# Second MLP, first pair of tiles: its output products as one single-precision matmul each, in an order found anew

## The chip, the cores and the metric

The kernel runs on one core of a Trainium2 chip. The metric is the device time of one execution in microseconds (us): the median of several runs, lower is better. The rows below come from one profiled execution, whose own time is given beside its span.

## The reference, cut to what matters

Attention over a causal window of 128 positions (4 batches, 8 heads, 576 positions, 64 per head) gives 2304 tokens of 512 numbers. A first MLP (512 to 2048 to 512, leaky activation with a slope for each hidden unit) and then the second MLP follow, all in single precision:

```
h = np.maximum(np.maximum(x @ w1, x @ w2), x @ w3)     # 2304 x 512 times 512 x 768, three times
return (h @ w_out).astype(np.float32)                  # 2304 x 768 times 768 x 512
```

## The kernel before

**Products of rounded parts.** TensorE takes operands in a rounded 32-bit form (`F32R`, shown as fp32r in the rows). To keep the precision, an operand is split in two: a rounded high part (ScalarE, a cast) and the rounded rest (VectorE or GpSimd, a subtraction), by the helper `split` (L519 to L524). A product is then three matmuls, high by high, high by rest and rest by high, added up in PSUM. Operands that are not split, those of the attention's scores (L872), transposes (L931) and values (L951, L968, L975), go to TensorE as plain single precision (`F32`).

**Second MLP.** `second_mlp` (L1082) goes through the tokens in tiles of `TILE` = 384, two tiles at a time, so there are three pairs (`p` = 0, 1, 2). The hidden products of a pair are block products (`product`, L1216) of 384 columns. For pairs 1 and 2 the output product is done by blocks too (`outs_by_blocks`). Only the first pair, p = 0, takes the plain way: `outs` (L1244) is called 18 times, for 2 tiles x 3 blocks of 128 tokens x 3 pairs of hidden chunks, and each call does two chunks `j` with three matmuls each, 128 tokens by 512 outputs. Its stationary operand is `g[j]`, the hidden values that `close` (L1435) splits when a maximum is complete. Its moving operand is `Wo[j]`, the output weights that `last_weight` (L1206) loads into a buffer of the ring `wt` and splits into one of the slots `WO_AT`.

**Attention.** `pair` (L812) handles two heads and 256 queries: 8 calls of the score matmul (L872), softmax on VectorE (L903), ScalarE (L909) and GpSimd (L921), 6 transposes (L931, the tiles `p` by the identity), a copy of the transposes from PSUM to the tile `pt` on ScalarE (L939), then the values (L951 reads `pt`), and a copy of the result (L998 or L983, ScalarE). Scores, transposes and values of most pairs share the ring `sb` of two PSUM banks, and `pt` is a ring of one. The last pairs run between the hidden products (L1034 to L1036) and output products (L1062) of the first MLP.

**Order.** Every operation is recorded by `plan.add` with an engine, a planned cost and its operands. `Plan.issue` (L137) then takes the operations in the order of a table of numbers, `ORDER`, and the DMA queue on SP and each engine get their instructions in that order. Between TensorE operations that the plan has early in the program, `keep_busy` (L161) puts fill matmuls (L461) on the identity; another 24 stand in the program from `pair` (L455).

Of the kernel before, what the change touches and what calls it, by code (L numbers as in the profile page):

```python
# [11 lines left out]
F32 = mybir.dt.float32  # L12
# [7 lines left out]
B, H, S, D = 4, 8, 576, 64  # L20
T = B * S
# [3 lines left out]
P = 128  # L25
# [3 lines left out]
NJ = DF2 // P  # L29
NC = NB // 2  # L30
N = 2 * P

R = 3 * D
# [56 lines left out]
class Plan:  # L90
# [162 lines left out]
    'c-'  # L253
    'jrqgJO_t007X>#$Ro<Y^)ZxW!tuG+qP}nwr$(CZQgs{;UGXka*zZNP!c2qB|tII9&ms`TaXfz1|0wc5(tn2Yy?Sx0}2FS7tkOk@E'
    '`^V0jWT05F5k-'
    'rNCTJ9E1V`o`N(W3}gUtfCX_u8ITF22k}5g5Dub1S#Sbm1_?lX5D5~3b^w5AkO<@j??6Y86{H1OKw^*$R0Ng5CXgLe0r|imPz_W7'
    'IY3TO3Df{pK^Kq<YytT}Zcqyp09!#5P#qKmdBA3{4MfA5U>;}+dV}qt4%iJMKwnTE3<UAu0#F<D2X#SbPzdY=MZgYF7}NvhKv9qm'
    '>;rv3H_#Jw0u4Y9&=2ec9btFS3p4{=L4D8=bcKUKb8r%j2HjvIFa$gUEx>*-'
    '01O51!C%lA3<58}7|;?72gAU8&>D;dAHg^P!3fX_j0Af?8!!bd1mnRduoOH8i@^af4J-mvL2|eZyaeUpbg&$p0-'
    'wMHa2iYkufP(p0!#$2!3;1NtORSpLGS?#hne9yFcXZ1v%xB`4!i-gz-llD`~zn|0=OO=1{XjLxCWdBhrk$k5o`dLz<F>7WI&$*fS'  # L260
    '17)a0JAMU%*vx6x;y!z%j5KR)h)RHE<Ig2VcQ0a2KS6iQshrVPkY3aCjTUfCy6f03?R7U^c`chDjiSS>Z$Q7zp?l#DrO3QWy!d!4'
    'Q}Oo`%_BE*J{)z})Z=cmi_5WH1Wmh2Ow;kPjAuv7v<dVP{wvhQT<n089ZDj0=lE3oF0~*a;SdHDM~~U{P2LriLwGCiDYn*b-'
    'KPt>91KVQbh1RffMn8)#s9I1@ERRbUSE8w9W!%mCZMs<1t52M?i)umdax7oje&1RMb~!D=uKY!2I@;;<(ShuvXG_#XC!y<rbn3Z6'
    '!NV0G9F)`p{CKez(cf&F1wH~<cYrC~WZ5)OoE;Sg8`4u#|4O4tz2Mq}Y1I1z@Rac~%%3@5>Ka0#3MZ=<>}Bbo~v!Fq5hTn4AYDR3'
    '2xMD<}~cm~ddP2e;*4`xTx;Vjq`E`qb+Ubq(Shcn<3v=Od{bKpU^8t#MZ;AXf6Zh{Bke7FIgg;D4PTmT!uCul3&0vE$*bP^ter(j'
    'NW2xdk*VH30vo`XlwHkb?DMcd&nm<8oV$6*+G2p_|za5uaT&!V#AGTZ?#!e?j?JP#kiCom7X3NOJ6@D)4^ufdP-'
    '2z&#tzz;Afc?R>M*RUFChTg&F(4(yAEqnow!cXu9Y>sZiyD%SWi(bNb<QBXK6>5P5VrUk+4JG;tOQQSmH%v}AYKiirX5=R<Pc-'
    '@rf5G;oJ*q+OK!d)(R_Hr?0AnMII-qYb25ODwkUua$4lPC<Q4!RFgrWkd6GEsf`T=91m}m~_j0&Q^up^m^FzSK|p*UzB`3DJ_hYl'
    'lvx*>{+q6icZL6jEtLWxj(G#{l$2~dBO7^OqKQ4$n}5~5-#DO!r+qN8X5+JH)<!l(pVN=l*PXdz04lA-SC3@U?;p&lqTT85ING-'
    'x?mjT)l*C<R(hj-#?D992c-'  # L270
    'P(_pyH9`YXd9(sGKwnS=v=LQCJy8|(6`eq9P#?4sT_TmxO(bbQv<jU>15jVI7TrO&&^J^KokG>oAXFQzL-$Y(^c3AkHBlXOg*-'
    'r4&{R|x4M)?FrlV0UG!zX+_0UK(3{68r&_gr>jY6^T2o!?HpiSr;dW6=a@8}cSf^L)ZXft|@V$!i_BD#P+qjBgex`?)-'
    'N$5Gcgx;d@=o;FFCZiqbF4>MIpq=O^x{fZRUnqo5L9y`*6qnpUp*R`cg_4n%C<fk*-'
    'l09{6^e=Dlh^1y+Kb+x4=4pmK|i95cpo}|%8~u(AWBKXZ~_t+S0F!7LXr<xB<W}-'
    'oQV8J2>(F<8=M>eMUglf=fM!CBL7e&f^ifkI5iPCGfqq>mN*VhPc3FR4M~f;&?KZQRX855PMYCFnBxRE3)Z+fPJ$iIi{s<UBpXhQ'
    'b6}6t;jB0zu7zuooH#oUa4wt_N8n^Q6%Hp=NPe6ir^d-'
    '~Ez+E%!Bt6BoC0US9Y_mY2#>;*a5yf8E91hr1Wt)Z<07~?u1yNyqPQg~h)d$exDKg?OW~Hd9IlO<;PSXMu7aE5R-'
    '_K@M(dIaxH|4m%itQgHK~Ye;<C6CX@$q&y0{H#i0hHQxF2py+TwM1F6oTh<Mp^BZigG;dbksAjXRSLxD6hT+mSA~KOTU);`w9*9*'
    'et>k+>)BhU?=6q!-?Rmyv~}0q%~+;of*4?ty#IK6nM`Nr&P=xGPzN7vhO{FrJKW;;DENUPPwjTX-'
    '5Cf`{SpcnV%gCg2%(HC{z#;>CC_UV^)kS$H1ah}YuTcn$7O7L)n-'  # L280
    'GFd|A;7#}rxk?t`rT8|!Mpoiwcr`hOkK)~UIo^u@;+=RK{)e~YRrosDg*W3J_#WAUui+K=2HAs;<GuI<K8SDNJNP=jPu7rq_z(u<'
    'CV4>i<F({2K8#OdMGxR!^cLw&&*BgG2!4b=;%7J(eMlbQ%;X7vh)>}x<SG7z4ZVjS<4}4Y|HhWy$Fb=j{0Tey97FN~$DwcVY5a)1'
    '#GbyzXYe_E0l&flMdUHLh~MGl^fkVOW6&!&l*A_QF((mJldNPAp+u4}%E(}H8DGVUU?NCLN=PIzBm<2@EJ;N_;}|50#3YVnBdKXL'
    'iA!UVjMS5OG&>0)nP?yS1qWmZ=}Uj$T%;69LraqaBsa-Nc91+IKlzG>(48bN`H6Fof}{}1Ns5vF<QtBpg-LNzhJ@3!<U1Zp29UIL'
    'Ac>+yNC^^6hmoQr9Vtn6kq9!BW+ds!Xfl$_B(um^GKP*K@5p$Pfs7;X$yPFk3@5|r1X7<2rz6OAGJ<X+v&l$0kxV7K$s{t3OeUl0'
    'bTW!gA(_Yw(tvy*dq_jlkM^gHNMq83Tp;_&d2*DDr3c7Cl9wJPhe$qpgft~n=w5Q193%V4YjT=gB;#lg@|K(+XUKT^k-Q-'
    '%$pm_qOr{g*DRPc{B0WidI*IloeMxWfn|vjVa{7~eBem#v(ue#awP`={gG{BL$sh8C<f4BGqW=h{f&#jZ<fhYT0h)&rI-No~gHk%'
    '1&ZGtDdQykZp#$g!GLUX28%Ys5ix#6*XjNK@7NzHC3A%|Cr|0PwQj!*;WoT(ymKLVfX*pVf)}<9`dHRIZpp|GfT9a0$_2^vslsqF'
    'BXngvd%%ctI655e=qRnX|`kOYTjcGIbhrS?9Xni`LwxA1W1A3aaq-|*edXZ+PXK6dyigu<6X?uExwx)yVLOPgspl#@4`j;-'
    'EmuME6mA)j`=~McgKBHG@Qucygqc`bonvC6`ugGP3i{7PI=nr~_-lO+vBKnUep%3UUnwb8iOX)-'  # L290
    'UhywPQE~ClWa+;LJVoxY#p)7>0p_t{MMHy#=#b%NfV}h-qj6t@NDu!4hrkQ6cST<@{P8u-FlCV`YJB`5-'
    'vy;@Z)ifq6&Qh|q^b}3Ya<c4f3(dvSuy?c-'
    '%fZ4~1{T3uvvh17O~ul)^)wSp%{I_NEF+6#8)*ranZ2h`tT4;MHq)%E2s=Wf*$4WGZlY~iHujNzrX|@?x|JTIFX?ewiS41~SRGc6'
    ')n(&Y8Fqq}W#d@|R-Tn&_1QLBk+o&b*>+lmRc5bfX%>goU@h1V+LG<2ujvH#hVG<QSxxqq)?(FII~K-'
    'v(b}v!i_3Dec&sz)&IYnUtRrjBy0T6zKI_1`vAuL6>%zX!!E7|k!+Nj=Y#;5(#<09>Ec;6Pvi-Cl>%|Vx-'
    's~VfOeeAatRd^e2Czo#5S_}Fv88M_o5rTI$!sQ@!Pc|oY!;is=CV0#9-Gg;(T!{aYseR{1Z*K|!56W`>^oh;HnB#$F;B>v@Xf3#-'
    '@;n)X1pce#+vhdtN?4xx3V3q4bRWEvkts1Z^ygyovc3}!iMo(Y&UDqJMvDvGk;;a@E*J?@5%SDUVI?$#s~1;ybmwPM)2W$DC^6|@'
    'uqALAI2K9!F(j2%7^e#ya^l1`|)OMG#|sq^O0-'
    '<pUCI(;cOD0%tx^4d<mbzr}43T1|P*{@>zTZo6Xno`FtK<z!&mmd=X#D=kUdRIp54z@RfWmTgO+jReU#J%h&S(auu5<H}KVLFWbl'
    'u@vVFlU&FTW)qES@!w1TBY&+k}ckq3Du-wOX@<VKh+|N(({p<jrE)TGw@*um&kMP5MkUYYU@?HEOKgMUu<NPq2A&;^X{205*PqNe'  # L300
    'eI6KSF@DuDLKgZAW2mBJhz%TPt><Yiiukp+5JiExQ^B4Ry8zFD8vuv2W!LP94@;$%BZ?FsOHXkJ~v61o-'
    'zsVl*Gwcq3$?vnP>=i%9?($jkF~7$juxso#yU#!HXY3<?!mqR0@*(@qpYqrI4tvJm@aOC<`^4Y!@$xOZ$KLTd@)7&TKl2ytF?-'
    'JE${+kEf5N!<!r!r{>?{AmUNRu&$u$y+_v{s0AV*6lg!sm#m@i+muj~VxD1WmzY^j_iKeBJ^6Z0YvNc`es<RA8%ua)1~PWhRQmFw'
    'gW_LE`$hyP-KIpJ6=lz-WBIa$UQE94ZZ_##R9KekvB0eBoiMVQbW@|7|MM|_oJJfSdroMeLY2~zNwT=MlYj9b1$CK8E7EUtv(Q>E'
    'vdWWeL{5WZE$<1xer8OpVY&6mkIe4|Xv<MX84hy>h<ggl8jBNOo?JQ+{L<BF6bIZrB5@OUB(k13LglsvhJCE|<JJVa#Vsl;lTT7>'
    'fiB0{7QX?c3SS%!*mk%_0{nMGQWfp3$Me2a|WxkP4uR;Cb9e7oEsqj`Ffg=Y}EWLAD&W)$f}7Lir#k(oqpaZctD-'
    '((??jb{^kWu(Z?vx_KkLH?9^MGl@r<P#U=KADr36nS~HC@k`eBI1b5&2x(VG8fO!3y6IDfGjGCiN5NRJSa<vJiN3hE)K~uqM|4vc'
    'FP*#s4OcE%YveuxGb;80=&F9CV$BW;<)@R3-'
    'X7ulBg`2i<;tutRSk0+M<@IDjv&|@{z128j3pNs;n*w@mI33I3??fm!^rRC$7m?rm1KlZplWXy*Mqe%h$4-xFP?^R-&b-'
    'FPe#)^1Cd|Z_7{ehwLEwi952RD8lc`*5ZroB-'  # L310
    ')7XqO)i#?#Uivfa)n;$|tgm7_54UuHwENDte2jvYmJ!Kg&L%zZf8%$)fy?94ns7uX3O$#^1^pa*7zJ28lm%u;?q^$w6wE7%r&#E8'
    'oj;Vu%20gfOZ&{~)27Am)gVlBw~+si^`ft4i>Z0;`E)ln7Om1XrU4QPYG_lSNxKS0q-`g;euIY_(X-'
    '5c7psW5i6cKqObQgi@=;LJ_EvT&qQ*pDM)@sTiui+9YDC*&?BerIv_YVyRdr+NtGYjaVT<)G)PHtP?B69JOAQ=9@)QwMA?Y2SpsU'
    'QLGYMMVLyWwuv%)yGW*Xh?8Qsh^zLBOlqIlBjTwGV!s%!!qrZ3Kt!q$Duv3S;;XdkhDfOrs6!%^IxM2pDUnl^<wwLBky;%U<@i}~'
    'Or%pq)H!inq*13uggP(UtBaz5O0O=7`{Jg!B`%9-bz7VeS44SUNM%qR)E$voT@}woMs-aLQQ1`mo<$8+S=BpHP(2WL#dYyeWK;J<'
    'E;U~jR*%Fnm0LX)PsBHoM?Dp#)C-'
    'YUy%euRQT19>RDVTjHCH_oZ$v&dPgUfVRWVhGzZb>T2eClqSCv!=byAg4AH`cyQhgUyR9Ur9{Sf~IkW5xppG0L|PJI^T)lcz7R8v'
    's?5><Ew#pQ1y<X2H$A^Ar*DJ7Ol)>K4>N-'
    'd47p%ThKR^?t&Sxd!`F=aI#OU9A0Wr(!0wn{9+WJ(!V#*^`7gsi6$$t1EmPax~6q%xVzEK|wkGPO)2Yw+|kTsBl0WLlX~rjsdTCY'
    'f8-'  # L320
    'QIWE#ijrAmA(>TXlZ{k%nL{>HIc2nLtn$d_s+7ztYw~=uu*@%u$XdLp9H|P(VltO3C|jyZvbe0TO2`&!l&UF9%QCX8Y^9p0a<aUv'
    '%}dILvVt6=D$6Res;tAS$=0f(9H+*r>awM*C2Ppqa*C=W+o<uXuB;~~sQR*l9IYD3iE659EStzls;R8Yo5@A0m7J!U%X<8jnyebg'
    '*7CHPu9m1Ca<S^DW~er@t7<Dd%2jHn>Lk0V`h2PCt~RR9a+d0$R;y*Ivzo1rt4^wc+N64_cCx2ju1=_4s+ZiQx~Mg(0q-'
    'JLsP?jjT&p&#-m<Igt#+%Gs+;Vi)~R!<x$Yy^tG=?O?kBgX4Qi+AF1M=wa+^A%_NeV@uiBvwt9|OM+OMvt^Xh;)sxGL5>Z-'
    'b^j;L$uy1K1ysGI7Lx}$EXyXum<te&WQs;R!On(4>tfqJT1=&AaldZUW!N2-'
    ';6rrxRN>V<l%UaD8>gL<vrtG4>1YOUMpPpXZcre|oNr|ZwEub!#r>Sg+i`l04&sJ|+yzp0;UzMiGOtHB!S+4`4KdWc@GyJ?|U>fd'
    'UP?ygtsJ-UmIsaNRs`j1+y*J-'
    'W$=~x=;uDZYet2*dan&=q%pQ1WMchpQT(VcWJ&9%{?+UoWCfnKVej<0*`&U&NXpoi+%x{pq#z22nb=oGq#4s-'
    '&&K!@q!db3`rlk0@Kr;e)=>6CheUZmsc0Xnfxr3dM~I*DGR2kO*1sotme>svaFKA_j?F?yt)pu_brJxZt3WAza|QIFGGbOwD;kJi'
# [1340 lines left out]
```

## Time and profile before

| | us |
|---|---|
| median of 3 runs | 772.17 (771.73 to 773.33) |
| the profiled execution: its time | 773.07 |
| the profiled execution: its span, first to last instruction | 771.3 |

The page of the profile gives the busy time of each engine as a share of the span: TensorE's matmuls (PE) 98%, its weight loads (PEld) 86%, VectorE (DVE) 75%, ScalarE (ACT) 58%, GpSimd (POOL) 37%. Matmuls are pipelined: a row's duration reaches past the start of the next matmul, so that what one matmul costs is read from start to start.

### The profile page before, as it was taken

The page shows a single profiled execution, that of the slowest core. Times are in us where ns is not written, and L with a number is a line of the kernel's source. Part 1 is how long each engine was busy: PE and PEld are TensorE (multiplying, and loading weights), DVE is VectorE, ACT ScalarE, POOL GpSimd, SP SyncE. Part 2 cuts the span into 40 slices and gives each one's busy share as a digit, 9 for nine tenths or more (in the row PEclk, how much of TensorE's full clock was granted, in tenths as well). Part 3 has the DMA queues.
Part 4 walks back from the last instruction along what each step waited for, and adds up shares of the span by engine and source line. Part 5 has one row for each costly group of instructions (what it writes and reads, how often), then busy time and mean ns, then how long its engine had stood idle before and what let it go on. Part 6 is the DMA issues. An engine that isn't in the chain of part 4 may idle for free.

```text
span 771.3 us, 17302 instructions
## 1 busy us (share of the span) xinstructions
PE 756.8 (98%) x6018; PEld 664.8 (86%) x6022; DVE 575.8 (75%) x1457; ACT 447.8 (58%) x1235; POOL 284.5 (37%) x385
## 2 busy tenths in 40 slices
PE   7899999999999999999999999999999999999998
PEld 4689877878777789988888888899998999999997
DVE  6999989987566689979785759669865676824574
ACT  5999867766454546468865756455445434422251
POOL 5655647667545344366553413413332200000000
PEclk9999999999999999999999999999999999999999
DMA  9877556555655476366877936787986999697502
GB/s 305 287 237 240 181 176 245 169 200 188 212 182 178 162 239 215 91 197 182 267 226 242 374 130 222 286 292 263 355 290 218 288 368 387 191 313 240 192 2 83
DMA packets 93096, 175.75 MB, mean 228 GB/s; under 512 B 11088, under 2 KB 53712, under 8 KB 93008
## 3 DMA queue, kind: packets, MB, share of 16 engines
q1 hardware_dynamic: 92544, 174.11, 68.3%
q8 instruction: 48, 0.79, 0.5%
q10 hardware_dynamic: 464, 0.53, 0.3%
q14 instruction: 40, 0.33, 0.1%
HBM read 120.33 MB, written 54.26 MB: 226 GB/s over the span
## 4 chain that ended last, share of the span: by engine, by line
PE 94%; ACT 3%; DVE 1%; DMA 1%; issue 0%; ACTq 0%; DVEq 0%
PE xb L1062 15%; PE sb L1225 13%; PE hb L1225 13%; PE xb L713 6%; PE hb L1034 5%; PE sb L679 5%; PE hb L679 5%; PE hb L1035 5%; PE hb L1036 5%; PE xb L1349 4%; PE sb L951 3%; PE hb L713 3%; PE sb L713 3%; PE sb L931 3%; PE sb L872 2%; PE xb L1250 2%
## 5 line engine op out<-in xcount | busy, mean ns | idle before, releaser
L1062 PE MATMUL xb<-g,w_a 128*128 128x512 f32 (+1 forms) x624 | 125.2, 347 | 0.6 <-DVE z L903 0.6
L1062 PEld LDWEIGHTS xb<-g,w_a 128*128 128x128 f32 x624 | 97.5, 189 | 18.5 <-issue 5.9
L921 POOL TENSOR_SCALAR p<-p,z 128x192 f32<-128x192 f32 x144 | 75.0, 536 | 67.3 <-DVE z L917 64.3
L1034 PE MATMUL hb<-x_a,w_a 128*128 128x512 f32 (+1 forms) x208 | 73.5, 353 | 0.6 <-DVE x_a L1000 0.6
L909 ACT ACTIVATE p<-p,z 128x192 f32<-128x192 f32 x144 | 64.6, 452 | 12.0 <-DVE z L903 11.3
L1035 PE MATMUL hb<-x_a,w_a 128*128 128x512 f32 (+1 forms) x208 | 70.9, 341 | 0.0
L1036 PE MATMUL hb<-x_a,w_a 128*128 128x512 f32 (+1 forms) x208 | 70.8, 340 | 0.0
L514 POOL TENSOR_TENSOR v<-v,p 128x192 int32<-128x192 int32 (+1 forms) x72 | 41.5, 579 | 63.2 <-DVE v L511 23.1
L1225 PE MATMUL sb<-w_e,w_a 128*128 128x384 f32 x282 | 54.8, 335 | 0.0
L514 POOL TENSOR_TENSOR wt<-wt,w_b 128x512 int32<-128x512 int32 x32 | 43.0, 1346 | 30.5 <-issue 9.7
L1225 PE MATMUL hb<-w_e,w_a 128*128 128x384 f32 x258 | 51.0, 334 | 0.0
L523 DVE TENSOR_TENSOR w_a<-wt,w_a 128x512 fp32r<-128x512 f32 (+1 forms) x60 | 43.8, 733 | 8.7 <-ACT w_a L521 6.7
L1013 ACT CAST g<-hb 128x512 fp32r<-128x512 f32 (+1 forms) x52 | 25.2, 486 | 42.2 <-DVE hb L1043 39.9
L1225 PEld LDWEIGHTS sb<-w_e,w_a 128*128 128x128 f32 x282 | 49.4, 188 | 0.2
L521 ACT CAST w_a<-wt 128x512 fp32r<-128x512 f32 (+1 forms) x78 | 42.9, 563 | 9.8 <-DVE wt L563 4.0
L713 PE MATMUL xb<-g,w_a 128*128 128x512 f32 x192 | 46.8, 389 | 0.0
L1034 PEld LDWEIGHTS hb<-x_a,w_a 128*128 128x128 f32 x208 | 39.4, 189 | 7.2 <-issue 1.9
L1225 PEld LDWEIGHTS hb<-w_e,w_a 128*128 128x128 f32 x258 | 45.1, 188 | 0.2
L1040 DVE TENSOR_SCALAR t<-hb,alpha_sb 128x512 f32<-128x512 f32 (+1 forms) x52 | 32.3, 621 | 15.7 <-PE hb L1036 15.2
L903 DVE CUSTOM_DVE_ANT_0 p<-sb,rel 128x192 f32<-128x192 f32 x112 | 35.3, 353 | 11.1 <-PE sb L872 4.9
L1036 PEld LDWEIGHTS hb<-x_a,w_a 128*128 128x128 f32 x208 | 39.4, 189 | 4.5
L1225 PE MATMUL hb<-w_e,x_a 128*128 128x384 f32 x222 | 43.1, 335 | 0.0
(293 smaller groups left out, 1934.0 us busy)
## 6 DMA issues: line engine op xcount, KB each, us to landing
w_a<-left SPq DMA_DIRECT2D x30, 512.0 KB, 5.1
x_a<-left SPq DMA_DIRECT2D x24, 512.0 KB, 5.2
w_b<-in_w_in SPq DMA_DIRECT2D x16, 512.0 KB, 6.1
w_b<-in_w_out SPq DMA_DIRECT2D x16, 512.0 KB, 5.1
left<-w_a SPq DMA_DIRECT2D x15, 512.0 KB, 4.2
qkv<-in_qkv SPq DMA_DIRECT2D x44, 160.0 KB, 3.0
p<-in_w SPq DMA_DIRECT2D x36, 192.0 KB, 3.1
v<-in_v SPq DMA_DIRECT2D x32, 192.0 KB, 2.9
```

The lines of the kernel that those rows point to most:

```text
L514: add("pool", 0.08 + n / 430, due - 5, lambda: nc.gpsimd.tensor_tensor(out=wt().bitcast(I32), in0=wt().bitcast(I32), in1=words(0), op=ALU. ...
L521: add("act", 0.05 + n / 1100, due, lambda: nc.scalar.copy(w()[:, 0, :n], of()), r=[of], w=[w])
L523: add("pool" if pool_lo else "dve", 0.08 + n / 430 if pool_lo else 0.07 + n / 960, due + 1, lambda: eng.tensor_tensor(out=w()[:, 1, :n], i ...
L679: nc.tensor.matmul(to(), w()[:, a, ws], xs[k]()[:, b], start=(first and at_m == 0), stop=(last and at_m == 5), skip_group_check=True)
L713: nc.tensor.matmul(bs[m](), W_out[f]()[:, a, cols], g[f]()[:, b], start=(opens and f == fs[0] and not a and not b), stop=(closes and f == ...
L909: exps.append(add("act", 0.45, due - 10 + a, lambda i=i, n=n, p=p: nc.scalar.activation(out=part_of_p(p, n), in_=part_of_p(p, n), func=AF. ...
L921: z.readers.append(add("pool", 0.4, at_a + 0.2, lambda i=i, n=n, p=p: nc.gpsimd.tensor_scalar(out=part_of_p(p, n), in0=part_of_p(p, n), sc ...
L1034: nc.tensor.matmul(to, wi()[:, 0, ws], x[:, 0, cols], start=(kk == 0), stop=False)
L1035: nc.tensor.matmul(to, wi()[:, 1, ws], x[:, 0, cols], start=False, stop=False)
L1036: nc.tensor.matmul(to, wi()[:, 0, ws], x[:, 1, cols], start=False, stop=(kk == KD - 1))
L1062: nc.tensor.matmul(to, wo()[:, a, ms], g()[:, b, :n], start=(opens and not a and not b), stop=(closes and ends), skip_group_check=apart)
L1225: nc.tensor.matmul(to()[:, :TILE], Qs[q]()[:, a, ws], x[:, b], start=(first and n == 0), stop=(last and n == 5), skip_group_check=True)
```

## The change

In the first pair's output products, `Wo[j]` becomes a plain F32 tile that the DMA fills directly, with no buffer of `wt` and no split. The hidden values `H` are copied by ScalarE in full precision, with no second part. `outs` issues one F32 matmul in place of three rounded ones, and the cost that the plan is told for a call goes from 6 x 0.2265 to 1.7. The table `ORDER` is replaced: it now lists 4139 operations instead of 4163, in another sequence nearly everywhere, though most operations move by a few places. The fill matmuls of L461 are 19 where they were 17.

```
-        wt = wt_r.new()
-        add("sp", 0.9, due - 8, lambda: nc.sync.dma_start(out=wt(), in_=w_out2_d[j]), r=[w_out2_b[j]], w=[wt])
-        Wo[j] = w_s.new(WO_AT[j], 0)
-        split(wt, 512, Wo[j], due - 3, j % 2)
+        Wo[j] = w_s.new(WO_AT[j], 3)
+        add("sp", 0.9, due - 8, lambda: nc.sync.dma_start(out=Wo[j]()[:, 0], in_=w_out2_d[j]), r=[w_out2_b[j]], w=[Wo[j]])
...
                 for j in js:
-                    for a, c in ((0, 0), (0, 1), (1, 0)):
-                        nc.tensor.matmul(o(), g[j]()[:, a, b * P:(b + 1) * P], Wo[j]()[:, c],
-                                         start=(j == 0 and not a and not c), stop=(j == NJ - 1 and a == 1),
-                                         skip_group_check=True)
+                    nc.tensor.matmul(o(), g[j]()[:, 0, b * P:(b + 1) * P].bitcast(F32), Wo[j]()[:, 0],
+                                     start=(j == 0), stop=(j == NJ - 1), skip_group_check=True)
...
-            add("pe", 6 * 0.2265, due, fn, r=r, w=[o])
+            add("pe", 1.7, due, fn, r=r, w=[o])
...
-                    split(T[at_], TILE, h, due + 2 * six + 2, True)
+                    add("act", 0.05 + TILE / 1100, due + 2 * six + 2, lambda h=h, at_=at_: nc.scalar.copy(
+                        h()[:, 0, :TILE].bitcast(F32), T[at_]()), r=[T[at_]], w=[h])
```

The new table is shorter, so that every line after it has another number in the changed kernel: 7 less up to `second_mlp` (L872, L931, L951, L1062 before are L865, L924, L944, L1055 after), L1225 is L1216 and L1250 is L1240.

Three places show what the order does on TensorE. The first is the first call of `outs` in the second MLP. A row is a line, an operation, the tile written and the tiles read, the size of the result, and how often it follows itself; the output goes to `xb`, the blocks of the hidden product to `hb` and `sb`. Before:

```order
L1225 MATMUL hb_7681<-w_e,x_a 128x384 x6
L1225 MATMUL hb_7710<-w_e,x_a 128x384 x6
L1250 MATMUL xb_7741<-w_a,g_7603 128x512 x3
L1250 MATMUL xb_7741<-w_a,g_7652 128x512 x3
L1225 MATMUL hb_7762<-w_e,w_a 128x384 x6
```

After:

```order
L1216 MATMUL sb_7585<-w_e,w_a 128x384 x6
L1216 MATMUL hb_7662<-w_e,w_a 128x384 x6
L1240 MATMUL xb_7673<-w_d,g_7596 128x512
L1240 MATMUL xb_7673<-w_d,g_7660 128x512
L1216 MATMUL sb_7616<-w_e,w_a 128x384 x6
```

A call of `outs` is two matmuls instead of two times three, between the same kind of neighbours.

The second place is near the end of the attention: on TensorE, what stands between a pair's scores (L872, after: L865), the transposes (L931, after: L924) and the values of the transposed pair (L951, after: L944). Before:

```order
L872 MATMUL sb_4464<-qkv_4288 64x192
L872 MATMUL sb_4467<-qkv_4288 64x192
L931 MATMUL sb_4519<-ident,p_4401 128x128 x3
L931 MATMUL sb_4523<-ident,p_4404 128x128 x3
L1062 MATMUL xb_4542<-g_4275,w_a 128x512 x2
L1062 MATMUL xb_4543<-g_4275,w_a 128x512 x2
L1062 MATMUL xb_4544<-g_4275,w_a 128x512 x2
L1062 MATMUL xb_4545<-g_4275,w_a 128x512 x2
L951 MATMUL sb_4561<-pt_4536,v_4301 64x64 x2
```

After:

```order
L1028 MATMUL hb_4486<-x_a,w_a 128x512
L1029 MATMUL hb_4486<-x_a,w_a 128x512
L924 MATMUL sb_4520<-ident,p_4383 128x128 x3
L924 MATMUL sb_4524<-ident,p_4389 128x128 x3
L944 MATMUL sb_4540<-pt_4532,v_4315 64x64 x2
L944 MATMUL sb_4543<-pt_4532,v_4315 64x64 x2
```

The twelve hidden products now stand ahead of the transposes, where the scores stood directly before, and the eight output products between transposes and values are gone. Transposes followed directly by the values that read their copy stand once more some 80 rows ahead of this (`sb_4308`, then `pt_4318`); before, there is no such pair.

The third place follows directly: the next transposes behind these values. Before:

```order
L951 MATMUL sb_4561<-pt_4536,v_4301 64x64 x2
L951 MATMUL sb_4564<-pt_4536,v_4301 64x64 x2
L1062 MATMUL xb_4542<-g_4275,w_a 128x512
L1062 MATMUL xb_4543<-g_4275,w_a 128x512
L1062 MATMUL xb_4544<-g_4275,w_a 128x512
L1062 MATMUL xb_4545<-g_4275,w_a 128x512
L931 MATMUL sb_4602<-ident,p_4505 128x128 x3
```

After:

```order
L944 MATMUL sb_4540<-pt_4532,v_4315 64x64 x2
L944 MATMUL sb_4543<-pt_4532,v_4315 64x64 x2
L924 MATMUL sb_4579<-ident,p_4503 128x128 x3
L924 MATMUL sb_4583<-ident,p_4513 128x128 x3
L1055 MATMUL xb_4588<-g_4275,w_a 128x512 x2
L1055 MATMUL xb_4589<-g_4275,w_a 128x512 x2
```

The four output products that stood between the values and the next transposes now stand behind the transposes.

## Rows read from the trace of the kernel before

**Rows 1.** The page: span, busy time of each engine.
```profile
span 771.3 us, 17302 instructions
PE 756.8 (98%) x6018; PEld 664.8 (86%) x6022; DVE 575.8 (75%) x1457; ACT 447.8 (58%) x1235; POOL 284.5 (37%) x385
```

**Rows 2.** Busy time by stretches: from:to, length, engines with instruction counts, granted clock.
```profile
core 0: us, PE busy (x) PEld busy (x) DVE busy (x) ACT busy (x) POOL busy (x), PEclk, DMA share, GB/s
0.00:20.00 20.00, 14.99 (x146) 8.22 (x149) 13.61 (x80) 11.67 (x44) 10.10 (x31) 1.00 0.94 308
20.00:40.00 20.00, 17.54 (x244) 12.40 (x246) 18.21 (x65) 20.00 (x71) 12.17 (x19) 1.00 0.84 276
40.00:60.00 20.00, 18.81 (x289) 16.54 (x285) 18.13 (x66) 18.87 (x63) 11.80 (x19) 1.00 0.68 223
60.00:130.00 70.00, 70.00 (x830) 57.76 (x829) 64.44 (x196) 59.82 (x181) 39.68 (x51) 1.00 0.64 210
...
560.00:600.00 40.00, 40.00 (x204) 36.41 (x203) 26.50 (x50) 19.61 (x46) 11.36 (x11) 1.00 0.80 260
```

**Rows 3.** The same view of L1250, L872 and L931 alone, whole span.
```profile
0.00:771.30 771.30, 25.46 (x108) 20.20 (x108) 1.00 0.69 228
...
0.00:771.30 771.30, 32.26 (x576) 19.71 (x576) 1.00 0.69 228
...
0.00:771.30 771.30, 30.98 (x216) 25.25 (x216) 1.00 0.69 228
```

**Rows 4.** Timeline of TensorE, output products: start, duration to the last end, line, count.
```profile
573.97 1.52 PE L1250 MATMUL sb<-w_a,w_e 128*128 128x512 f32 x6
575.33 1.98 PE L1250 MATMUL hb<-w_a,w_e 128*128 128x512 f32 x8
```

**Rows 5.** Timeline of TensorE: scores of 64 by 192, four at a time.
```profile
36.66 0.33 PE L872 MATMUL xb<-x_c 64*64 64x192 f32 x2
36.67 0.33 PE L872 MATMUL xb<-w_c 64*64 64x192 f32 x2
...
37.15 0.33 PE L872 MATMUL xb<-x_c 64*64 64x192 f32 x2
```

**Rows 6.** Timeline of TensorE: six transposes between rounded products.
```profile
246.80 0.39 PE L1036 MATMUL hb<-x_a,w_a 128*128 128x512 f32 x1
247.03 0.81 PE L931 MATMUL sb<-ident,p 128*128 128x128 f32 x6
247.60 0.48 PE L1034 MATMUL hb<-x_a,w_a 128*128 128x512 f32 x1
247.92 0.40 PE L1035 MATMUL hb<-x_a,w_a 128*128 128x512 f32 x1
```

**Rows 7.** Timeline of TensorE at the attention's end; idle time before in brackets.
```profile
259.11 0.83 PE L872 MATMUL sb<-qkv 64*64 64x192 f32 x16
261.20 0.85 PE L931 MATMUL sb<-ident,p 128*128 128x128 f32 x6 [1.26 <-DVE z L903]
...
263.81 0.34 PE L951 MATMUL sb<-pt,v 64*64 64x64 f32 x8
...
264.66 1.20 PE L1062 MATMUL xb<-g,w_a 128*128 128x512 f32 x4
```

**Rows 8.** Timeline of ScalarE: copies of transposes (L939) and of results (L983).
```profile
248.13 0.84 ACT L939 COPY pt<-sb 128x384 f32<-128x384 f32 x2
...
262.52 0.83 ACT L939 COPY pt<-sb 128x384 f32<-128x384 f32 x2
...
264.98 0.41 ACT L983 COPY o<-sb 128x128 f32<-128x128 f32 x2
```

**Rows 9.** Groups on GpSimd, 500 to 592 us: the second parts.
```profile
L523 POOL TENSOR_TENSOR g<-p,g 128x384 fp32r<-128x384 f32 x6 | 7.1, 1177 | 3.6 <-ACT g L521 3.5
```

**Rows 10.** What TensorE waited for in the first 60 us.
```profile
PE xb L872 <- DVE w_c L840: 4.9, 1, 4.9
```

**Rows 11.** Timeline of TensorE where the first MLP's last products end.
```profile
334.37 0.38 PE L623 MATMUL hb<-ident 128*128 128x512 bf16 x1 [0.77 <-DVE g L1014]
```

More of the change, by code (lines that the diff above doesn't have):

````diff
@@ L260 @@
[L260 to L264, printed above, removed]
@@ new lines @@
+    '`Q9Bl!pCq4=l}0%#uTf-stox}n3U2uh6-p;(jz6-9|re?(9yN`rc#1qh-'
+    '9C>2VEC`yVFqNS)9N{&jQ(x@;BM`5TpT1tweWoQHHj!K{?v>f$73sD&qfmWb1XgN8GHlj!rjT)l*=ongwZlaW^Dk_T_p%kbADu*h'
+    'f7*rk&M3qqmbR2y_eNYwD6MaP|P$je)^+T6PUnFTYGyttaC($`{2c1H<P<2!rtwG<=Q*;jvLTk|#av!ZjHBcS&09`>-QB5=yO-'
+    'GuJM0L?{G#Cv-wa_#)8r4HX&?qzmokt^3T)ZAVL}O4e-h{@YiRe4}gf^oK=r(zT#-'
+    'Xd|B8o$|pwH+rx`ei(@n{lyjwYjP=q=iYCZHYYI=YO0qPt`Y+KINKU+4u&NN%7I91n++mnfX>Lc#PM3c|0@ZnOs_Ca=+Z6bHXSAJ'
+    'ATugp?y6Q6x==lad2yA3BJVk^LwEPKbY?NRkgHClyF4nu4UqztLax2LWtwZj5jS97XbAh%@16@(*F05fdzMMUs-'
@@ new lines @@
+    'l$C<IkX(+|9SmG|!VTKj%N)us^IS$3ma1xvtYn%)>$9ZuU9KgwOC6WUt#i?**QWb~ctT-'
+    'Fag>&N6I2=deDkK6&<4}?YXUCDaI?0b?NJ^X*Hz(a_3S14x;O?{*Zh=eSBDgZHgbU$OxEL;stK-qQIIfMWk^;CWZb?ewg19lRNlM'
+    '{zxC(AXYT!D!G_FOO;+D7!Zh~8r4x}tDk89!zxHf5p>*6+~6KROsl8U%J?u$F)F}NRYi`U_fxDIKD>*4jd6K;fC;|{np>4Mwf;kX'
+    '^?ihJVzcmS@CyWw8A3mJ<?;0Cxm9*KM7x}*oLNBZD#crF=;H{fNYE9pUd(xG@Eo=+CxZe${!jBnyecq*QbZ{aC;5FUod<7s#SnTa'
+    'Rh8F)3Gg;$Wlcrl)hm*BOyJK2cW;30Spo{KM&d3Yt6j~9|ncmZCDZ{t;D8D2zI;-mN&-'
+    'invw?f5U=iMQd^WH<hYci|Oy72b?@;HzX0-'
@@ new lines @@
+    'hOku}GGaY8J{2TTLxX&Q4O#R#C?SEQl3naaam=ims)xEGNs(a<Lrj9ZktvvD7SvZJ}vdYnFyZu~aOYt)uB!A-'
+    '0~TXC+u>_MT>7g;^H1ffivI*%7*texRG_Cz_RIVr|$anvH#=pJ_>Ulpdom>2X?yZKdT{9affAVB=X`R*zL;6<K|@hmK?ASt(YTRb'
+    'i!Bb5?_Gqg7d3ww<<M)mTk-'
+    'g0^I}*bdr`?WV72byl10q_61&7M~4d9oZoEhIVDUXm{3$b!P3^TiT6vU|m=bHkgfOJy~CtfK6n%*%;Q3^<oKGe>Rr&W{KDU)`ul#'
+    'd+8TCiREGY=vSJTHDLScGPaaWX9wtHHkBQu)7W7;lg(yR*eo`K9ir=5LpFykXB$}~wt>xM4f#U0iOpk+*nHN4FJ=qaX10ZWqf6K}'
+    'wv{Dejd)|;gny?kc~jnsx8@!AcGiry;X7D!-km39ZFxIhfaPQTd4ATOcjTRTXTFmS<2`s6-'
@@ new lines @@
+    'LhuWf@UW9F_Tbagm3Y6(z($c}ezF$K)?rfL9XbL}gKs|CWd371=->mo-HdaYEjb<;7uHOH>sn<z-'
+    'o0Jd{^uHPKw$mes{6S%}vW*JNE$K|GeH<s*4rwik`WCDTyckgsGtanZC8jYUgwQx@jm<sI2Xe3sqB5BXZw7ac_r-a-'
+    '76t;Ai~RCE%}!~oS=+>@VVcQIJ?5S_(+*+%peJw;pbM81?=!~^+Mb`?c=FY!!%k;V8x^+paA&*dOBR=kyeWINGcypz4f3pqga5nt'
+    'td`Bx4T#rbey)D!{KKruq}6@$bFIZ_N3qXbkXxKkhHIDwQ^<HZDlRfrlQCW>idv><A#Xsad(s-'
+    '}xMBA%Ko#)uhWrif4_`7FUyKUIqNS6nR?$&^s5#U>$Duxh8~3a{piVQPU;YN42;lB<A<uV#zVe4YqWOT{9wM1(4>;;3aJfhxn}sx'
+    '>01+9eXI<zk&!A=ZjSYO~lP!qiF;sn(0FVz}BMwu!`Qqli%l#dZ;{MyORHg*qwHt0*-'
@@ new lines @@
+    'Q_kct`AvD###A>sO<R-8R4@fh4b#q))a^|{Q%V;yRZJ06)l@WvO$SrS)HFp+H8b8!F!fAFQ`vMfwM>08$xJl8Ol{NI)G-'
+    'ZAX+7E0HBC)-)5!ENWpr=T&@?ks%m~xd^fir57t_Q{HF-@})6euVSIreO*p$`%%`{U^4=@AG95dZ?Gb7DVGsFxsbIo-#-'
+    'wZP|%?wjs&og7paI?T%GqcQSv(!}3x6D{W?QOHr%r?u+YQyXzv(_v&74;gk#8lGD%{n9P3L|VD!);}~!HhC1%_?)mY&2E$db7oBG'
+    'MkOE+ssx|Ro^hXO*MVf>@db|H+#$hv(xM{+U_@xO?7?H>@`o!9dpPuv&YR{^U&1L`^-Ia!n`tP%p-'
+    'H(yf!C|vv15(bIQCm&rDPM+#EFzOmq9f95(OFOLNw|H>b@fQ&U@e-h4K-'
+    '^au0Bd^E?*H`Bs?H{PBzUk$K7OpyI+p#5oT>)+;|3D^|&m-%DrXk_QvI2K!CqitN9(ni@dHm$9z)7f~oo({GNZHSF;Q`s1s-'
@@ new lines @@
+    'p1MtHi=DOGucG8zRqk@+l)5cCbmg!7TZ8)wb^U~o89KH$!v1l(B`xewxtcV4RtPCz&6s2ZEjo8M%q@kkPWkqY!h49cC-'
+    '0xF<Zp8v-xcvThtb}-'
+    'E9fm+P1fOZDZZVwy|YwN!!+Tu%&EQTiQ0!9c?Gu)Aq8RZCTsb_ORt_72DfZwdL(7JJ9yC)$DxR$1bpgY$aRWR<Pr2EnCA@wzX|V+'
+    'ux41BWxX8({8bY?MPeKF0|uqJv+n>u=VXwJJwFL!|ZT7#!j%4>>|6wPPL2eQajl$vs>+SyTVShYwSup$4;@!?OMCauCsUT4m;P*w'
+    'A<|lJHy_xJMC?|+upIW>}osPZnV4XF}ufZvg_?WyVq{Bo9zL+-yXO3>;rqy9<ulC6Z_Dfv`6eCd)S_^XY31m)IPQu-BWwkW^vE#M'
+    '|;Yiv*+z|d(ob@FYO6;!Ctl}-'
+    '79;^ey~^UC3n@nwr}hg``KQzm)&)H!+y1&EOo!_P5ah<vw!S6``x~`*rj#M{jlkrbU!U|+1+3J%PRNG{j<Ocr(JpnT?WUUcgW>(&'
@@ new lines @@
+    'z*4rm)8|=A<jDIf?PZo$HjFoT|yV^Uby(~wM*m@xK}QjOYD-kP?y{#bvaxLm(zv2w=UX6xq>dt6>^zeN|)8ey3DSyi*QBU8&}j-'
+    'b}=r}opn`QDtFgqb0u7ESKOs``CKWN$K7`2T^cvum2(wc6L;O^ccon=SJf4B6<ilr(lv6`Tp3s0wR1Jy8Q0Zycg<W4cg^*1wOk$7'
+    '+f8u&Ty0m^^>X#yXxG;@cCB0k*U{B;BV9|^(2a37TnjhRwRR8ODc9CDb)#GxH_4TCr`<r;%{6y}++=sb4RAwT2RGEUcY|F|H^p6X'
+    '7hNYe)pd3^-7q)J-EmjlOxMRvceh-'
+    'BH^Yr}v)w~?&&_j>+;BI`jdKg#2)D@1ap&Az_t`CQ=iPj_*zI&n+!wdXEq80(W4F}3b1U3ex5h1V@7-#*(yenF-Fmmx-'
+    'FLg(Znwd0a@*Wy_rx7```lBv-yLvU+!6QD?Qz@P2lvVCbwAw>chE6^)ctbb-'
@@ new lines @@
+    '7$B_{dRxcH}}IGcmEvqe;x493y(eW+)Gcq_R1&p#wYRtZ@u$ze317(z7O_Ed|aQvC-)&fo=@zP`m{dOC-dWd8XxJy`~)BFqkIY<;'
+    'iG*@pWbKkF+SF(^BMePKh3A|8U0M3&u8<geSV+WXZMAC7N6DU@P&OPpVQ~^1$`c$+ZXUfd|qGFSN0`+F<;!5_N9CYU%{94Rec#>('
+    'bx3le0g8RSM#-eeP7*A^v!$?-_TF;Eqz^I+t=~UeFI<5H}Q>pW8cEJ@=g65Ki_xot^Fe3#&`5>eK+6ExA&cVci-7}@x6Rk-'
+    '`n@_eSBX((D(HHe1AXK5Ap;2EI-W8_Cx##KhzKRi~UN!#82^~{YXFEPxVXv3O~b-'
+    '@yq=(ztykuqx?4i(O>do{anA=FYp`uJU`Aa^lSVHzs_&++x=;O(qH#${Sm*zZ}ivvQUA$*@wfa=zu8~#$NWwI*`M;e{AItzulHyD'
+    'aeu>K^t=66f7S2v=lmXj#eehr{TaX4-'
@@ L363 @@
+    '}MLmd4Jm<@Q3_8|J^_Ihy4rx!@u<J{ZIeOKlYFOGylQg@lXAI|HQxc5Bzig+rRa{{9pgZ|MM{L&j0Zw00K0C12%vHfdC8eK-'
+    '_=|xPS-*1#}=d5HH{Z2?B8fG7u6lfh2)Mfuw=>fn<S%fv7<8Kv*DgAUqHehz^7XA_FM{F@Y3;*uZ~Zwsx='
 )
````

157 lines of the change are left out of this document (52 added, 105 removed).

## The prediction

> **What bounds the kernel now.** I read the page first. TensorE's matmuls are busy for 756.8 of 771.3 us, and no other engine for more than 75% of it [rows 1]. The view by stretches says where the missing 14.5 us are: TensorE stands idle for 5.0, 2.5 and 1.2 us in the first three stretches of 20 us, together 8.7, and is busy without a gap in the long stretch behind them as in the one that holds the output products of the first pair [rows 2]. So behind the first 60 us whatever is added to TensorE is added to the end, and what is taken from the other engines gives nothing, as long as TensorE goes on without waiting. Two places break the rule. At the end of the attention a group of transposes waits 1.26 us [rows 7], and where the first MLP's last products end a mark waits 0.77 us [rows 11]. In the first 60 us it is the other way round: ScalarE is busy for 20.0 of 20 us and then 18.9 of 20 while TensorE has gaps [rows 2], so there the order of the ScalarE work decides; 4.9 us of the 8.7 are one wait for the first data to have landed and been scaled [rows 10].
>
> The granted clock is 1.00 of full speed, the 2.4 GHz level, in all these stretches [rows 2]; TensorE does not become less busy by the change, so no term below has to do with the clock.
>
> **The change part by part.**
>
> *Rounded matmuls out.* 108 matmuls at L1250 go [rows 3]. Six of one call start at 573.97 and the next call at 575.33, so one costs 1.36 / 6 = 0.227 us from start to start [rows 4]. That is 108 x 0.227 = 24.5 us less on TensorE.
>
> *Single-precision matmuls in.* 36 matmuls of 128 by 512 come. The trace has none of this size in plain F32, but it has smaller ones. First, how many passes a call is: the score helper calls 8 matmuls for each of 36 pairs of heads, 288 in all, and 576 records stand in the trace; the transposes, 6 x 36 = 216 calls, have 216 records [rows 3]. So a plain F32 matmul is two passes, a transpose one. Then, what a pass takes: the scores, four quarters of the array at a time, start at 36.66 and after three more groups at 37.15, so a pass of 192 columns takes 0.49 / 3 = 0.163 us [rows 5], that is 0.85 ns a column, against 0.227 us / 512 = 0.44 ns for the rounded form. The transposes use the whole array as the new products will: six start at 247.03, a rounded product follows, and the one behind that starts at 247.92, so they take (0.89 - 0.227) / 6 = 0.11 us for 128 columns, 0.86 ns a column [rows 6]. For 512 columns the scores give 0.435 us a pass, with the rounding of the timeline 0.427 to 0.444. I take 0.43, towards the lower end, since part of a short pass is its start and does not grow with the columns. Two passes cost 0.86, and 36 of them 31.0 us (30.7 to 32.0). Switching between the kinds costs nothing: the transposes start 0.23 us behind a rounded product, as the next rounded one would [rows 6]. The net of the two parts is +6.5 us (6.2 to 7.5) on an engine that has no gap there.
>
> By the Trainium skill, page "FP8 and Floating Point Precision", section "TensorE Precision Notes", true FP32 goes through the array in four passes; four passes of the trace's 0.227 us would make the net 36 x 0.908 - 24.5 = +8.2 us. The trace shows two records a call, each with nearly twice the time of a column, which is a little less than that; the measured pass decides.
>
> *Splits out.* 12 subtractions for `H` on GpSimd (six of them 7.1 us together [rows 9]), 6 for `Wo` on VectorE and GpSimd, and 6 casts on ScalarE go; the 12 copies of `H` stay on ScalarE, in another type. GpSimd is busy for 11.4 of 40 us there, VectorE for 26.5, ScalarE for 19.6, and TensorE has no gap [rows 2]. I cost this at nothing: TensorE's own work covers it. If that cover were gone, at most the work of the last call's operands, one GpSimd split of 1.2 us [rows 9], would be won.
>
> *Output weights loaded straight into their slots.* Six DMAs of the same bytes, now waiting for the slot and not for a buffer of `wt`, on the SP queue ahead of some stores and loads. The operations that read the slots last belong to the first MLP, which is over when the first call of `outs` comes, so I cost it at nothing; a wait there would hold the loads queued behind on SP, and would show as a gap of TensorE between 500 and 560 us.
>
> *The order, at the end of the attention.* Here the new order takes away a wait and makes three. Taken away: the twelve hidden products, 12 x 0.227 = 2.7 us, now stand between the scores and the transposes that need the same two banks, and the wait of 1.26 us for VectorE's reading of the scores [rows 7] has cover. Made: values directly behind the transposes whose copy they read, twice. In the trace such transposes start at 247.03 and would be done issuing at 247.68; their copies end at 248.13 + 0.84 = 248.97 [rows 6, 8], so values that stood directly behind would wait 1.3 us. The other case of the rows, transposes at 261.20 and copies until 263.35, gives 1.5 [rows 7, 8]; with a ScalarE that starts at once, 247.84 + 0.84, it is 1.0. I take 1.3, the nearest case, since the exponentials of the next scores stand ahead of the copies on ScalarE in both. And transposes directly behind values whose two banks ScalarE must copy out first: values at 263.81, next matmul at 264.66, result copied by 264.98 + 0.41 = 265.39 [rows 7, 8], so 0.7 (at least the copy itself, 0.4). What is queued behind these waits is the whole of TensorE's program, in order, and no later gap takes it up. Sum: 2 x 1.3 + 0.7 - 1.26 = +2.1 us (2 x 1.0 + 0.4 - 1.26 = 1.1; 3.7 if the old wait also stays).
>
> *The order elsewhere.* In the first 60 us ScalarE's and TensorE's sequences are both changed. Of the 8.7 us idle 4.9 are the wait for the first data, so at most 3.8 can be won there, and a like amount lost; I take 0, and for the range 1.5 either way, an estimate of somewhat less than half of it. The two further fills cover a gap or cost 0.2 us each, inside that. The wait of 0.77 us may go or stay; I leave it.
>
> The sum: +6.5 + 2.1 = +8.6 us. The profiled execution would go from 773.07 to 781.7, its span from 771.3 to 779.9. The median shown, 772.17, is 0.9 below the profiled time; from it the forecast is 780.8.
>
> **The rivals.**
>
> *The new waits cost nothing.* ScalarE could have the copies ready sooner, and other work could close the gaps. Then only the old wait goes: 772.2 + 6.5 - 1.3 = 777.4. Against it: the values cannot start before their own transposes are copied, and that takes two ScalarE copies, 0.84 us [rows 8].
>
> *The order loses more.* Waits at the high price, 3.7, and 1.5 more in the ScalarE-bound start, where more ScalarE work could stand ahead of what TensorE waits for: 772.2 + 6.5 + 3.7 + 1.5 = 783.9.
>
> *Faster: a full-size plain matmul is one pass.* The whole-array matmuls of the trace in plain F32, the transposes, are one record each [rows 3]. If the new products were one pass of 0.43, 36 x 0.43 = 15.5, net -9.0, with the waits 772.2 - 9.0 + 2.1 = 765.3. It decides below (24.5 - 2.1) / 36 = 0.62 us a matmul. Against it: the scores, which are plain matmuls and no transposes, are two [rows 3]. A sharper form is that only columns count: then a new product costs 0.227 as a rounded one, net 36 x 0.227 - 24.5 = -16.3, and the time is 758. The Trainium skill, page "TensorE: Matmul & The Clock Gate", section "Back-to-back issue gap", gives the gap by the columns alone and names no type. By that rule the change would win; the trace disagrees, 0.163 us for 192 columns in plain F32 [rows 5] against 0.227 for 512 rounded ones [rows 4].
>
> **How the numbers follow.** A change under 0.2%, 1.5 us, could hardly be told from none. The forecast's case (new waits of 1 to 3 us) has 0.57, the waits that cost nothing 0.19, the order that loses more 0.16, the single pass 0.04 in both forms, and 0.04 is left for a better start that makes up the whole. The likeliest is 780.8, its own range 778.5 to 782.5. For the range I add the low ends, 772.2 + 6.2 + 1.1 - 1.5 = 778.0, and go 1 us below it to take in most of the case without waits; the high ends are 772.2 + 7.5 + 3.7 + 1.5 = 784.9, all at once, and I stop at 784.0. Slower 0.93, same 0.03, faster 0.04.
>
> **What would show it.** The passes: 72 records at the new products' line, 0.43 us apart, and some 31 us busy where L1250 had 25.5. The waits: idle time of TensorE ahead of two groups of values (on ScalarE's copy of the transposes) and of one group of transposes near 250 to 270 us, and no 1.26 behind the scores. Behind 340 us no gap. The splits: GpSimd's second parts on `g` and `H` gone, and nothing won. The forecast is wrong if the new products are one record each, if idle time turns up in the second MLP, or if the first 60 us have clearly more or less than 8.7 us idle.

## The result, and the profile after

The changed kernel takes 778.62 us (median of 3 runs, 778.45 to 778.70) against 772.17: slower, by a ratio of 1.008 with a 95% interval from 1.0057 to 1.0103. The forecast was 780.8 with a range from 777.0 to 784.0, so the sign and the range hold and the value is 2.2 us too high. The profiled execution of the changed kernel has the median's time, 778.62; that of the kernel before lay 0.9 us above its median. So the two profiles differ by 5.5 us and the medians by 6.45.

The page of the changed kernel, span and busy time of each engine, as in [rows 1]:

```profile
span 776.8 us, 17245 instructions
PE 763.7 (98%) x5988; PEld 658.5 (85%) x5988; DVE 567.8 (73%) x1454; ACT 445.5 (57%) x1229; POOL 269.3 (35%) x370
```

TensorE is busy 6.9 us longer; GpSimd is busy 15.2 us less and VectorE 8.0 less, and nothing of that is seen in the time. The new products alone, by the view of stretches for their line (L1240, before L1250, [rows 3]), and two rows of TensorE's timeline:

```profile
0.00:776.80 776.80, 31.88 (x72) 13.56 (x72) 1.00 0.68 226
```

```profile
583.03 3.60 PE L1240 MATMUL hb<-w_d,w_e 128*128 128x512 f32 x8
586.46 5.31 PE L1240 MATMUL xb<-w_d,g 128*128 128x512 f32 x12
```

36 matmuls leave 72 records, two each, as the scores did. Eight of them start at 583.03 and the next at 586.46, so a pass takes 3.43 / 8 = 0.429 us from start to start, a product 0.858, and all of them 72 x 0.429 = 30.9 us where 108 rounded ones took 24.5.

The stretches of [rows 2] again (columns as there), and what TensorE waited for, the longest waits of the whole span:

```profile
0.00:20.00 20.00, 15.07 (x175) 8.34 (x176) 13.25 (x79) 12.20 (x44) 10.67 (x32) 1.00 0.94 312
20.00:40.00 20.00, 18.57 (x251) 13.58 (x251) 18.67 (x70) 19.96 (x74) 13.95 (x21) 1.00 0.73 225
40.00:60.00 20.00, 18.74 (x256) 15.36 (x255) 18.93 (x65) 19.92 (x63) 11.54 (x17) 1.00 0.88 305
...
560.00:600.00 40.00, 40.00 (x144) 25.66 (x143) 22.13 (x46) 16.99 (x37) 4.52 (x7) 1.00 0.68 220
```

```profile
PE xb L865 <- DVE w_c L833: 4.9, 1, 4.9
PE sb L944 <- ACT pt L932: 1.2, 2, 1.0
PE sb L924 <- POOL p L914: 1.1, 2, 0.8
```

In the first 60 us the idle time is 7.6 us in place of 8.7; the first wait, 4.9, is the old one [rows 10]. In the second MLP TensorE still has no gap, as its stretch from 400 to 760 us shows (TensorE alone: busy, count, granted clock, DMA share, GB/s):

```profile
400.00:760.00 360.00, 360.00 (x1918) 1.00 0.74 253
```

The wait for VectorE's reading of the scores [rows 7] is gone, and so is that at the mark, the matmul on the identity (L623, after: L616) where the first MLP's last products end [rows 11]. Values (L944) now wait twice for the copies of their transposes, and transposes (L924) wait for the tiles `p`.

### The profile page after: what moved, and what is told of

It is laid out like the page before. It is cut to its first block, busy times and chain, and to the rows that moved or that the text cites. A ratio compares the mean times of both kernels' runs of the same rounds, so it can differ in the third digit from the quotient of the medians.

```text
span 776.8 us, 17245 instructions
## 1 busy us (share of the span) xinstructions
PE 763.7 (98%) x5988; PEld 658.5 (85%) x5988; DVE 567.8 (73%) x1454; ACT 445.5 (57%) x1229; POOL 269.3 (35%) x370
## 4 chain that ended last, share of the span: by engine, by line
PE 92%; ACT 3%; DVE 2%; DMA 1%; issue 0%; POOL 0%; SPq 0%; DVEq 0%; ACTq 0%
PE xb L1055 14%; PE sb L1216 13%; PE hb L1216 13%; PE xb L706 5%; PE hb L1027 5%; PE hb L1028 4%; PE hb L1029 4%; PE hb L672 4%; PE xb L1338 4%; PE sb L672 4%; PE sb L944 3%; PE hb L706 3%; PE sb L706 3%; PE sb L924 2%; PE sb L865 2%; PE xb L1240 2%
## 5 line engine op out<-in xcount | busy, mean ns | idle before, releaser
L1055 PE MATMUL xb<-g,w_a 128*128 128x512 f32 (+1 forms) x624 | 123.7, 347 | 0.5 <-ACT g L1006 0.3
L1055 PEld LDWEIGHTS xb<-g,w_a 128*128 128x128 f32 x624 | 97.5, 189 | 18.6 <-issue 6.0
L914 POOL TENSOR_SCALAR p<-p,z 128x192 f32<-128x192 f32 x144 | 76.8, 548 | 65.2 <-DVE z L910 56.4
L1216 PE MATMUL sb<-w_e,w_a 128*128 128x384 f32 x282 | 56.6, 339 | 0.0
L514 ACT CAST w_a<-wt 128x512 fp32r<-128x512 f32 (+1 forms) x72 | 39.3, 559 | 21.8 <-DVE wt L556 7.5
L1216 PE MATMUL hb<-w_e,w_a 128*128 128x384 f32 x258 | 51.6, 336 | 0.0
L1216 PEld LDWEIGHTS sb<-w_e,w_a 128*128 128x128 f32 x282 | 49.4, 188 | 1.5 <-issue 1.2
L1216 PEld LDWEIGHTS hb<-w_e,w_a 128*128 128x128 f32 x258 | 45.1, 188 | 0.5 <-issue 0.5
L556 POOL TENSOR_TENSOR ve<-ve,ve 128x256 f32<-128x256 f32 x16 | 12.5, 782 | 94.3 <-DMA ve<-x2d 94.3
L516 DVE TENSOR_TENSOR w_a<-wt,w_a 128x512 fp32r<-128x512 f32 (+1 forms) x57 | 36.9, 651 | 9.5 <-ACT w_a L514 5.3
L1216 PE MATMUL hb<-w_e,x_a 128*128 128x384 f32 x222 | 43.2, 336 | 0.0
```

The costliest lines, as they stand in the source:

```text
L514: add("act", 0.05 + n / 1100, due, lambda: nc.scalar.copy(w()[:, 0, :n], of()), r=[of], w=[w])
L516: add("pool" if pool_lo else "dve", 0.08 + n / 430 if pool_lo else 0.07 + n / 960, due + 1, lambda: eng.tensor_tensor(out=w()[:, 1, :n], i ...
L914: z.readers.append(add("pool", 0.4, at_a + 0.2, lambda i=i, n=n, p=p: nc.gpsimd.tensor_scalar(out=part_of_p(p, n), in0=part_of_p(p, n), sc ...
L1055: nc.tensor.matmul(to, wo()[:, a, ms], g()[:, b, :n], start=(opens and not a and not b), stop=(closes and ends), skip_group_check=apart)
L1216: nc.tensor.matmul(to()[:, :TILE], Qs[q]()[:, a, ws], x[:, b], start=(first and n == 0), stop=(last and n == 5), skip_group_check=True)
```

## The experiments

The kernel before ran on the same chip as each of them and took 772.11 to 772.45 us. Line numbers differ a little from kernel to kernel; the names of tiles do not.

### The products or the order

**The new products in the old order.** All edits of the change but one:

```
-ORDER = (the changed kernel's table)
+ORDER = (the table of the kernel before, without the 24 operations that are gone)
```

Two operations stand a little later in it, both DMA issues on SP: the loads of the first two chunks of output weights, 21 and 12 places further down the table.

> The changed kernel's arithmetic (plain products, no splits) in the order of the kernel before. Theory: the cost is TensorE's own, 36 products at 0.858 us in place of 108 at 0.227, +6.4 us, whatever the order; the old order has its old gaps, so the time is 6.4 above the kernel before, about 778.6, and no faster than the changed kernel (0 to 1 us above it, as the new order won about 1 us of idle time). Rival, the new order carries the loss and the plain products cost little: within 2 us of the kernel before. Rival, the recorded sum with 2.1 us for the new order: 2.1 us below the changed kernel.

Measured: 778.28 us, ratio 1.0083 (1.007 to 1.0096), that is +6.4 us. The new products' line reads as in the changed kernel, with its clock at 1.00:

```profile
0.00:777.90 777.90, 31.71 (x72) 13.58 (x72) 1.00 0.68 226
```

So the products alone cost what the whole change costs, and the two rivals fall. The run also bears on what the new order costs as a whole: the ratio is 1.008 with it and 1.0083 without, and the two intervals together leave some 2 us either way.

**Three rounded matmuls again, in the new order.** The low parts of `H` and `Wo` are left out of the result, and ScalarE's copy of `H` writes the rounded type; TensorE's work is that of the kernel before:

```diff
-                    nc.tensor.matmul(o(), g[j]()[:, 0, b * P:(b + 1) * P].bitcast(F32), Wo[j]()[:, 0],
-                                     start=(j == 0), stop=(j == NJ - 1), skip_group_check=True)
+                    for n in range(3):
+                        nc.tensor.matmul(o(), g[j]()[:, 0, b * P:(b + 1) * P], Wo[j]()[:, 0].bitcast(F32R),
+                                         start=(j == 0 and n == 0), stop=(j == NJ - 1 and n == 2), skip_group_check=True)
```

> The changed kernel's order and its missing splits, but each output product is three rounded matmuls again, all three of the same unsplit operands (the low parts of H and Wo are left out of the result). Theory: 6.4 us below the changed kernel, about 772.2, or up to 1 us below the kernel before, since the new order and the missing splits are all that differ from it. Rival, the new order costs 2.1 us: 774.3. Rival, the missing splits win time that the plain products hide: 2 us or more below the kernel before.

Measured: 773.38 us, ratio 1.0011 (1.0001 to 1.0021). That is 5 us below the changed kernel, and 0.9 above the kernel before where 0 to 1 below was expected. The rival of 774.3 lies outside the interval, and so does a gain from the missing splits. Its profile has one wait that the changed kernel's has not, in the second MLP; TensorE's timeline, and then ScalarE's:

```profile
597.72 1.34 PE L1216 MATMUL sb<-w_e,x_a 128*128 128x384 f32 x6 [1.11 <-ACT sb L1232]
```

```profile
595.81 1.48 ACT L514 CAST w_a<-wt 128x256 fp32r<-128x256 f32 x4 [1.00 <-DMA wt<-w_out]
597.19 0.47 ACT L1232 COPY sb<-hb 128x384 f32<-128x384 f32 x1
```

The copy for which TensorE waits stands in ScalarE's queue behind casts, and the first of these waited 1.00 us for a load of weights. In the changed kernel the same copy waits for TensorE, and the same product comes later; TensorE and then ScalarE:

```profile
603.01 1.20 PE L1216 MATMUL sb<-w_e,x_a 128*128 128x384 f32 x6
```

```profile
602.22 0.46 ACT L1232 COPY sb<-hb 128x384 f32<-128x384 f32 x1 [0.43 <-PE hb L1216]
```

Without its wait TensorE would be at this product 603.01 - (597.72 - 1.11) = 6.4 us sooner than in the changed kernel, which is the whole price of the plain products; the load is not there so soon, and 5.3 are left. Why the kernel before, with as much TensorE work in the old order, has no such wait is not shown.

**The splits kept.** The kernel before, with only this changed (the low parts are made and not used):

```diff
-                    for a, c in ((0, 0), (0, 1), (1, 0)):
-                        nc.tensor.matmul(o(), g[j]()[:, a, b * P:(b + 1) * P], Wo[j]()[:, c],
...
+                    nc.tensor.matmul(o(), g[j]()[:, 0, b * P:(b + 1) * P].bitcast(F32), Wo[j]()[:, 0].bitcast(F32),
```

> The kernel before, in its own order and with all its splits, and only the three rounded matmuls replaced by one plain one of the two high parts (the low parts are made and not used, so they are left out of the result). Theory: the splits lie beside TensorE's work, so it is as slow as the plain products in the old order without splits, +6.4 us above the kernel before (5.7 to 7.1), 778.7. Rival, the splits hold up TensorE: 2 us or more above that.

Measured: 778.31 us, ratio 1.008 (1.0066 to 1.0094). Without the splits, in the same order, it was 1.0083. GpSimd has all its old work again and the time is the same:

```profile
PE 762.1 (98%) x5982; PEld 657.8 (85%) x5986; DVE 576.0 (74%) x1457; ACT 447.2 (58%) x1235; POOL 284.3 (37%) x385
```

**Every new product twice.** `for n in range(2)` around the plain matmul, into the same bank.

> The changed kernel with every plain output product issued twice into the same bank (the result counts each product twice). Theory: 36 x 0.858 = 30.9 us above the changed kernel, about 809.5, and 144 records. Rival, half of a plain product's time is a cost of starting a call or of switching, which a second product of the same operands doesn't pay: 15 to 25 us. Rival, TensorE is not the bound in that stretch: less than 15 us.

Measured: 808.66 us, ratio 1.0476 (1.0461 to 1.049). By the two ratios that is (1.0476 - 1.008) x 772.1 = 30.6 us above the changed kernel. The products' line, twice as many records and twice the time:

```profile
0.00:806.50 806.50, 62.77 (x144) 27.24 (x144) 1.00 0.65 218
```

In its timeline a pass is as far from the next as before: eight start at 581.83 and the next at 585.26, 0.429 us each. So the whole price is per pass; nothing of it is paid once for a call.

### The pieces of the order

**The old order at the attention's end.** The changed kernel, and of its table only the 285 operations of this stretch in their old order.

> The changed kernel with the order of the stretch at the attention's end (285 operations, planned 223 to 269 us) taken from the kernel before; nothing else differs from the changed kernel. Reading of the trace after: the three new waits are 0.24, 1.00 and 0.77 us, the old one 1.26, so 0.7 us below the changed kernel. The recorded sum: 2.1 us below it. Rival, the old wait in this place is as long as the three new ones together: no difference.

Measured: 777.90 us, ratio 1.0067 (1.0053 to 1.008). The stretch can be read by itself: in both kernels the same scores stand at its start and the mark behind its end, and only the order between them differs. TensorE's timeline of the changed kernel, and then of this one:

```profile
243.06 0.83 PE L865 MATMUL sb<-qkv 64*64 64x192 f32 x16
...
335.80 0.39 PE L616 MATMUL hb<-ident 128*128 128x512 bf16 x1
```

```profile
242.53 0.83 PE L844 MATMUL sb<-qkv 64*64 64x192 f32 x16
...
334.07 0.39 PE L595 MATMUL hb<-ident 128*128 128x512 bf16 x1
```

From scores to mark are 92.74 us with the new order and 91.54 with the old: the new one costs 1.2 us there, between the 0.7 and the 2.1 that were expected. In the five other runs with the changed kernel's order in this stretch it takes 92.75 to 92.79, so this is no scatter. But the time fell by less. In the second MLP TensorE now reaches one product too early: it waits for a ScalarE copy that stands behind a cast, and the cast waits for a transfer out of its buffer `g`. TensorE and ScalarE in the changed kernel, and then in this one:

```profile
629.01 1.20 PE L1216 MATMUL hb<-w_e,x_a 128*128 128x384 f32 x6
...
627.69 0.51 ACT L514 CAST g<-wt 128x384 fp32r<-128x384 f32 x1 [1.12 <-DMA rightT<-g]
```

```profile
628.63 1.34 PE L1195 MATMUL hb<-w_e,x_a 128*128 128x384 f32 x6 [1.03 <-ACT v L1207]
...
627.69 0.51 ACT L493 CAST g<-wt 128x384 fp32r<-128x384 f32 x1 [2.70 <-DMA rightT<-g]
```

The cast starts at 627.69 in both, though TensorE is earlier in one. Without its wait TensorE would be 629.01 - (628.63 - 1.03) = 1.4 us ahead of the changed kernel here; with it, it is 0.4 ahead. So 1.0 us of this lead is not paid out.

**The new order in the first stretch alone.** The kernel before, with 770 operations of its table, from the 23rd on, in their new order.

> The kernel before, with its rounded products and splits, and only the order of the first stretch (770 operations, planned up to 93 us) taken from the changed kernel. Reading of the trace after, in which the first 60 us have 7.6 us idle in place of 8.7: 0.5 to 1.0 us below the kernel before. The recorded term of 0: no difference.

Measured: 772.20 us, ratio 0.9999 (0.999 to 1.0008): no difference that can be told.

**The mark later.** The same, and two groups of output products moved ahead of the mark. TensorE's order (without the numbers, that kernel against this one):

```
-L595 LDWEIGHTS ident
-L595 MATMUL hb<-ident 128x512
 L1034 MATMUL xb<-g,w_a 128x256
...
 L1034 MATMUL xb<-g,w_a 128x256 x2
+L595 LDWEIGHTS ident
+L595 MATMUL hb<-ident 128x512
 L651 MATMUL hb<-w_a 128x512 x6
```

> The kernel before (rounded products, splits) with the changed kernel's order in the first stretch and, where the first MLP ends, two groups of output products (12 matmuls of 256 columns) moved ahead of the mark that waited 0.77 us; the rest in the old order. Theory: the wait is covered, 0.8 us, and the start gives 0 to 0.5 as in the run of the start alone: 771.2 to 771.7, 0.1 to 0.2% below the kernel before. Rival, the wait comes back at the next product behind the mark: no difference.

Measured: 772.48 us, ratio 1.0003 (0.9994 to 1.0011). The rival was right. The mark has no wait, and the next product has one of 0.66 us, for a ScalarE copy of the bank:

```profile
334.93 0.39 PE L595 MATMUL hb<-ident 128*128 128x512 bf16 x1
335.98 1.66 PE L651 MATMUL hb<-w_a 128*128 128x512 f32 x6 [0.66 <-ACT hb L664]
```

### What less work on TensorE would have won

Two of the rivals had computed how much faster the kernel would get if a plain product were cheap. That can be tried with rounded matmuls of the unsplit operands, one or two a product, in the changed kernel: `range(1)` and `range(2)` in the edit shown above. The low parts of `H` and `Wo` are left out of the result.

> The changed kernel with one rounded matmul in place of each plain one, of the same unsplit operands (the low parts of H and Wo are left out of the result); order and splits as in the changed kernel. Theory: a plain product is two records of 0.429 us and a rounded one a single record of 0.227, all of it on the path, so 36 x (0.858 - 0.227) = 22.7 us below the changed kernel, about 755.9. Rival, the columns alone count: no difference. Rival, the loads or ScalarE take over as the bound of that stretch once TensorE is faster: 5 us or more of the 22.7 are missing, as gaps of TensorE between 525 and 600 us.

> The changed kernel with two rounded matmuls of the same unsplit operands in place of each plain one (the low parts of H and Wo are left out of the result). If TensorE bounded the stretch: 36 x (0.858 - 0.454) = 14.5 us below the changed kernel, 764.1. Theory after the run with one: the work of the other engines between 525 and 600 us ends no earlier, so it is about as fast as one rounded matmul and as three, 770 to 772.5, with gaps of 2 to 7 us in that stretch.

Measured: 771.53 us with one (ratio 0.9991, 0.9982 to 1.0) and 772.61 with two (1.0001, 0.9991 to 1.0012). TensorE has 22.7 and 14.5 us less to do than in the changed kernel, and the time falls by 7.1 and 6.0. With one, TensorE's waits and the stretches (TensorE alone: busy, count, granted clock, DMA share, GB/s):

```profile
PE sb L1216 <- ACT hb L1232: 8.4, 1, 8.4
...
PE xb L1241 <- ACT g L1442: 3.5, 1, 3.5
```

```profile
560.00:580.00 20.00, 16.49 (x78) 0.91 0.76 229
580.00:600.00 20.00, 11.64 (x56) 0.74 0.81 252
```

With two, one wait of 6.7 us stands in the same place. The rival that the loads or ScalarE take over as the bound was right, and so was the theory of the second run: with one matmul, of 22.7 us 11.9 come back as these two waits, and 3.7 of the rest as a lower clock (last section).

**The copy first.** In the run with one rounded matmul the copy for which TensorE waited 8.36 us is `COPY hb<-sb` on ScalarE, behind casts that wait for loads. ScalarE's order, that run against this:

```
 L514 CAST w_e<-wt 128x384 x2
+L1249 COPY o<-xb 128x512
+L1249 COPY o<-xb 128x512
+L1249 COPY o<-hb 128x512
+L1232 COPY hb<-sb 128x384
+L1249 COPY o<-hb 128x512
 L514 CAST w_a<-wt 128x256
-L514 CAST w_a<-wt 128x256
-L1249 COPY o<-xb 128x512
...
-L1232 COPY hb<-sb 128x384
```

> The run with one rounded matmul a product, in which TensorE then waited 8.36 us for one ScalarE copy out of a bank (and 3.51 for a cast), with that copy moved ahead of the seven ScalarE casts of the next weights that stood before it in ScalarE's queue and waited for their loads; one rounded matmul of unsplit operands as there (low parts left out of the result). Theory, ScalarE's queue in its order holds the copy back: the gap of 8.36 shrinks to 1 to 3 us, the clock of 580 to 600 us comes back from 0.74, and 5 to 9 us are won, 763 to 767. Rival, the loads and casts themselves bound that stretch whatever their order: the wait comes back within the next 20 us and the time stays within 2 us of 771.5.

Measured: 772.25 us, ratio 0.9992 (0.9981 to 1.0002). My theory fell and the rival holds. The wait is 7.90 us; ScalarE's timeline shows the new holder, and what SP's queue waited for longest from 570 to 592 us is the next link:

```profile
584.90 0.59 ACT L1228 COPY o<-hb 128x512 f32<-128x512 f32 x1 [3.58 <-DMA out<-o]
585.51 0.46 ACT L1211 COPY hb<-sb 128x384 f32<-128x384 f32 x1
```

```profile
SPq L1244 <- DVE wt L535: 4.5, 2, 3.8
```

The copy of an output must come first, since it empties the very bank `hb`; it waits until a store has left its buffer `o`; and ahead of the stores on SP's queue stands a load whose buffer VectorE had not yet left. That the one wait hands on to the other is read from the order of the queues and was not tried. No engine is full there, by the stretches of this kernel (PE, PEld, DVE, ACT, POOL, clock, DMA share, GB/s):

```profile
570.00:580.00 10.00, 5.26 (x24) 3.87 (x22) 6.59 (x12) 4.44 (x10) 0.83 (x1) 1.00 0.69 222
580.00:590.00 10.00, 3.97 (x12) 3.70 (x12) 4.73 (x11) 5.10 (x13) 2.15 (x3) 0.66 0.62 203
```

It is a chain of few buffers and in-order queues, and one move only handed the wait to the next link. Which link would have to give (a third buffer `o`, another order on SP) was not tried and stays open.

## Why the prediction was right, and where it was off

*The products.* +6.5 was forecast, +6.4 measured: two records a product, 0.429 us a pass where 0.43 was taken. The step that carried it, a price per column read from short plain matmuls [rows 5, 6] and two passes read from counted records [rows 3], holds, and doubling the products shows it from the other side. The forecast said that nothing in that stretch hides it; there is no gap, and the price is the same in either order.

The Trainium skill, page "TensorE: Matmul & The Clock Gate", section "Wait — 56ns, not 53.3ns?", gives 426.7 ns for 512 columns while the array runs at its lower clock. The trace has 0.429 us for a plain pass with a granted clock of 1.00, the 2.4 GHz level; so here it is the plain form that costs twice the time, and not the clock.

*The splits and the slots of `Wo`.* Nothing was forecast and nothing came: 1.008 with the splits and 1.0083 without, and no gap of TensorE from 400 to 760 us in the changed kernel.

*The attention's end.* The sign was right and the size was not: +2.1 forecast, +1.2 measured from scores to mark, and less than that in the time. The three waits are where they were forecast; TensorE's timeline of the changed kernel, then ScalarE's and GpSimd's:

```profile
242.32 0.34 PE L944 MATMUL sb<-pt,v 64*64 64x64 f32 x8
...
246.68 0.81 PE L924 MATMUL sb<-ident,p 128*128 128x128 f32 x6
247.74 0.66 PE L944 MATMUL sb<-pt,v 64*64 64x64 f32 x5 [0.24 <-ACT pt L932]
...
248.77 0.33 PE L865 MATMUL sb<-qkv 64*64 64x192 f32 x1
...
262.17 0.34 PE L944 MATMUL sb<-pt,v 64*64 64x64 f32 x8 [1.00 <-ACT pt L932]
...
263.87 0.95 PE L924 MATMUL sb<-ident,p 128*128 128x128 f32 x6 [0.77 <-POOL p L914]
```

```profile
247.21 0.86 ACT L932 COPY pt<-sb 128x384 f32<-128x384 f32 x2
...
261.26 0.86 ACT L932 COPY pt<-sb 128x384 f32<-128x384 f32 x2
...
263.13 0.43 ACT L976 COPY o<-sb 128x128 f32<-128x128 f32 x2 [0.82 <-PE sb L944]
```

```profile
262.59 1.62 POOL L914 TENSOR_SCALAR p<-p,z 128x192 f32<-128x192 f32 x4 [6.01 <-DVE z L910]
```

The first was costed at 1.3 and is 0.24. The step that failed took the copies' start from a case in which ScalarE was late, 248.13 for transposes at 247.03 [rows 6, 8], and let the values wait for both copies. Here ScalarE began 0.53 us behind the transposes' start, and the first values started 0.53 behind that, when the first of two copies was done. The second is 1.00 (1.3 forecast); there ScalarE began 0.91 behind the transposes at 260.35. The third is 0.77 (0.7), but for another reason than the one forecast, so that the agreement is luck: the copies of the result are done at 263.56, and the transposes start at 263.87, when GpSimd has written the tile `p` that they read. That GpSimd writes `p` between softmax and transposes stood in no term of the sum.

These waits sum to 2.0 against the old 1.26, that is 0.75, and the stretch lost 1.2. Idle time alone reads too little: the values behind the first wait go on at 247.74 but wait again for the second copy inside a row. They take 248.77 - 247.74 = 1.03 us up to the next scores, where the same values at 242.32, which had no wait, take 243.06 - 242.32 = 0.74. That is 0.3 of the missing 0.45.

*The mark and the start.* The mark's 0.77 us, "left as is", are gone in the changed kernel. That a single move in the old order brought 0.66 of them back one product later shows that the new order covers more than that one wait. The first stretch was set at 0 ± 1.5: the scores that start at 243.06 after had this start before:

```profile
243.41 0.83 PE L872 MATMUL sb<-qkv 64*64 64x192 f32 x16
```

That is 0.3 us won up to there in these two profiles, but the runs scatter by more: these scores start between 241.88 and 243.61 in the other runs with the new start, and at 243.12 and 244.11 in the two with the old one. The 7.6 us of idle time in the first 60 us are 7.5 to 8.35 in the other runs with the new start. The run with the new start alone can't be told from the kernel before, so a gain from the start is not shown.

*The sum.* 6.4 + 1.2 - 0.8 - 0.3 = +6.5 us, 778.7 by the median of before, where 778.62 was measured. So close a fit is partly luck: the terms of the order are read inside single profiles, those of the kernel before and after differ by 5.5 us as a whole, the 0.3 is not shown, and the run with the old middle shows that a gain ahead of the second MLP is not paid out in full. Without these readings, the ratios of 1.008 with the new order and 1.0083 with the old say that the order as a whole has no cost that can be told, where the forecast had +2.1, at the edge of what the two intervals leave. That term makes nearly all of the 2.2 us by which the forecast was too high; 0.1 comes from the products.

*The rivals.* "The new waits cost nothing" (777.4) is 1.2 us too low and the forecast 2.2 too high: the waits are there, but other gaps closed. The figures of the faster rivals, 765.3 and 758, were wrong in a step that didn't reach the forecast. They took what TensorE saves as saved time. The rounded run with one matmul a product is the sharper rival itself, and it takes 771.5. A gapless TensorE shows that added work is paid in full; it doesn't show how much of a saving would be paid out. The part of the prediction that read "whatever is added to TensorE is added to the end" was safe, its mirror image was not.

## What to carry to other kernels

Count the records of a call before taking a price from its duration, and price a long form by the columns of a short one: that made the main term here to within 0.1 us. Where an engine is busy without a gap, work added to it costs its full price, but for work taken away look at what the others have to spare: here TensorE's 14.5 or 22.7 us less gave 6.0 or 7.1, and a gain of 1.4 us met a wait of 1.0 that the changed kernel's profile doesn't have. Values set directly behind the transposes whose copy they read, in a new order, cost 0.5 and 1.0 us here; the price hangs on what ScalarE has queued ahead of the copy, so it is read from the queue of that place and not from another pair's.

## What was not expected of the hardware

After the idle 8.36 us of the run with one rounded matmul TensorE came back slower. Its timeline there, products of 384 columns, and then the same form in the changed kernel:

```profile
589.30 2.29 PE L1216 MATMUL sb<-w_e,w_a 128*128 128x384 f32 x6 [8.36 <-ACT hb L1232]
591.39 2.12 PE L1216 MATMUL hb<-w_e,w_a 128*128 128x384 f32 x6
593.31 1.29 PE L1216 MATMUL sb<-w_e,w_a 128*128 128x384 f32 x6
```

```profile
599.89 1.20 PE L1216 MATMUL sb<-w_e,w_a 128*128 128x384 f32 x6
600.93 2.24 PE L1216 MATMUL hb<-w_e,x_a 128*128 128x384 f32 x12
```

The six behind the gap take 591.39 - 589.30 = 2.09 us, 0.348 each, against 600.93 - 599.89 = 1.04, 0.173 each, in the changed kernel. That is half the speed, the 1.2 GHz level, and the granted clock of the stretch is 0.74. The stretch of the 3.51 us wait, 560 to 580, has 0.91. So a saving that leaves a gap gives part of itself back: with one matmul a product TensorE's records take 744.7 us in all, only 19.0 less than in the changed kernel instead of 22.7:

```profile
PE 744.7 (97%) x5948; PEld 654.7 (85%) x5952; DVE 568.1 (74%) x1454; ACT 445.5 (58%) x1229; POOL 272.1 (35%) x370
```

By the Trainium skill, page "TensorE: Matmul & The Clock Gate", section "Part 1: The HAM clock gate (the "warmup" mystery)", an idle array falls back to 1.2 GHz; the trace agrees, with 0.348 us behind the gap against 0.173.

The other thing is how little room stands behind a TensorE without gaps. With three rounded matmuls TensorE would have reached one product 6.4 us sooner than in the changed kernel, and with the old middle another one 1.4 us sooner; it then waited 1.1 and 1.0 us for a ScalarE copy that a transfer held back. The changed kernel's profile has no gap at either place.
